# Attention and mixture-of-experts kernel: value products as two 64-key matmuls on two row tiles, value splitting over two groups, list tiles with a step of 2

## The chip, the cores and the metric

The kernel runs on one core of a Trainium2 chip, as one program. The metric is the device time of one execution in microseconds (us), lower is better. Besides the plain runs there is one execution taken with the hardware profiler; its rows are what the text argues from. The engines are called as the profile calls them: PE (matrix multiply), PEld (its weight loads), DVE (vector), ACT (scalar), POOL and SP (mostly issuing DMAs).

## What is computed

```python
# B, S, D = 8, 2496, 256; z is (B, S, 64); E = 8 experts, F = 1024
scores = z @ z.transpose(0, 2, 1) / S
out    = np.maximum(scores, 0.0) ** 2 @ v
x      = (u * out).reshape(B * S, D)
logits = x @ w_gate                       # (B*S, E)
# greedy: the (token, expert) pairs in falling order of logit; a token takes the first expert
# that has room left (capacity B*S/E = 2496 rows each)
y[rows of e] = np.maximum(x[rows of e] @ w1[e], 0.0) @ w2[e]
```

All products are made with float32 values split into a high and a low part of type fp32r (a reduced float32 that PE takes in one pass), three matmuls for each: high by high, high by low, low by high.

## The kernel before

**Attention, the first part.** A batch has 2496 queries and as many keys. Queries go in 5 groups of 512 (the last of 448), keys in 20 tiles of 128 (the last of 64). One pass of one group over one key tile is a *step* here; a group has 20 steps, the stage 8 x 5 x 20 = 800. The steps are numbered through, n, and one loop (lines 967 to 986) writes the program: at step n it writes the scores of step n+4, the square of n+2, and so on, and work that is due now and then is held in a table, `todo`, under the number of the step (lines 913 to 952). For a step:

- `scores` (L782), every fourth step for four key tiles at once: z has 64 columns, so these matmuls contract over 64 rows, and two of them are written one after the other for the upper and the lower 64 rows of the PE array, into two PSUM banks. Three such pairs make the scores of two key tiles; a visit of `scores` is 6 pairs, 12 matmuls.
- `rectify` and `square` on ACT (tiles r, a), `split_hi` (tile hi; for three steps of five on ACT, for two on DVE, L803) and `split_lo` (tile lo, DVE, L812).
- `av` (L825, L827, L828): for each half d of v's 256 columns three matmuls over all 128 keys, vh by hi, vh by lo, vl by hi, into the bank `acc{d}`. There are two banks of each d, so that a group writes one while the other is read. The last step of a group has 64 keys and needs no lo of its own; it has two matmuls for each d.

At a group's end `take_acc` copies the two banks to SBUF (`at0` on ACT, `at1` on DVE, L836 and L834); two steps on, `turn_back` (L848) turns them on PE with 8 transposes over all 128 rows; `post_mul` (L859, tile xs) multiplies by u; and `post_logits` (L876, tile lt) makes the gate's logits on DVE, 32 instructions for each group. For the next batch z is turned (`z_turn`, two transposes each, 5 times in a batch's third group) and v is split into vh (ACT) and vl (DVE) by `split_v` (L763, L764), one key tile in each step of the batch's last group. [...] After the eighth batch comes the second part.

**Routing and experts, the second part.** Expert by expert, a threshold search (`hist`) finds the rows of the expert, the list of these rows is built, rows are gathered, and the two layers run on PE. The list of an expert is a product of one-hot tiles (`oa`, `hl`, `ob` in `route`): for each of 156 columns one matmul (L431) whose stationary operand is `obs[c][:, n, :, r]` and whose moving operand is `hl[:, n, :, :, r]`. The tiles have the columns in runs of QW = 4 innermost, so that DVE can work on runs; PE thus reads every fourth element of a bfloat16 tile. The routing of expert k+1 is written between the matmuls of expert k.

**What sets the order.** The engines each take their own instructions in program order. That order is not the order in which the Python loop calls: the tile framework sorts instructions when it builds the program, within what data and buffers allow. So the place of an instruction on its engine is read from the built program.

Of the kernel before, what the change touches and what calls it, by code (L numbers as in the profile page):

```python
# [8 lines left out]
F32 = mybir.dt.float32  # L9
# [4 lines left out]
AF = mybir.ActivationFunctionType  # L14
# [81 lines left out]
def moe(tc, xd, first, jp, identf, w1, w2, out, B, S, cp):  # L96
    nc = tc.nc
# [22 lines left out]
    with ExitStack() as ctx:  # L120
# [77 lines left out]
        nc.vector.tensor_copy(idl, idh_i)  # L198

        CB = JP // 4  # L200
        QW = 4
        QN = CB // QW
        slot = rp.tile([128, 128, QW], BF, name="slot")
        nc.gpsimd.iota(slot, pattern=[[1, 128], [0, QW]], base=0, channel_multiplier=0,  # L204
# [444 lines left out]
def attention(tc, u, v, z, w_gate, xd, identf, made, first, scale):  # L649
# [15 lines left out]
    with ExitStack() as ctx:  # L665
# [8 lines left out]
        def load_gate():  # L674
            wgb = wk.tile([128, E, D], F32, name="wgb", bufs=1)
            for h in range(2):
                wg = wk.tile([128, DH, 128 * E // 2], F32, name="wg", tag="xs")
                wg = wg.rearrange("p a b -> p (a b)")
                nc.sync.dma_start(wg, bass.AP(tensor=w_gate.tensor, offset=w_gate.offset + h * 128 * E,
                                              ap=[[0, 128], [1, 128 * E]]))  # L680
                with in_turn(0):
                    nc.vector.tensor_copy(wgb[:, :, h * 128:(h + 1) * 128], wg.rearrange("p (d e) -> p e d", e=E))
            wgt = wk.tile([128, DH, E], F32, name="wgt", bufs=1)
            nc.sync.dma_start(wgt, w_gate.rearrange("(h p) e -> p h e", h=DH))
            WG.update(rows=wgb, cols=wgt)
# [83 lines left out]
        def width(g):  # L769
            return min(512, S - 512 * g)  # L770
# [43 lines left out]

        def av(n):
            b, g, kt = seq[n]
            if kt == 0:
                ACC[b, g] = [ps.tile([128, 512], F32, name=f"acc{d}") for d in range(2)]
            last = kt == NT
            h, l = HI.pop(n), LO.pop(n, None)  # L820
            for d in range(2):
                o = ACC[b, g][d][:, :width(g)]
                c = slice(d * 128, (d + 1) * 128)
                vh, vl = VH[b, kt][:, c], VL[b, kt][:, c]
                nc.tensor.matmul(o, vh, h, start=(kt == 0), stop=False)  # L825
                if not last:
                    nc.tensor.matmul(o, vh, l, start=False, stop=False)  # L827
                nc.tensor.matmul(o, vl, h, start=False, stop=last)  # L828

        def take_acc(b, g, d):  # L830
            t = wk.tile([128, 512], F32, name=f"at{d}", bufs=2)[:, :width(g)]
            o = ACC[b, g][d][:, :width(g)]
            if d:
                nc.vector.tensor_copy(t, o)  # L834
            else:
                nc.scalar.activation(t, o, AF.Copy)  # L836
            AT[b, g, d] = t

        def turn_back(b, g):
            for half in range(2):  # L840
                p = ps.tile([128, 512], F32, name="sc", bufs=SCB)
                for i in range(2 * half, 2 * half + 2):
                    c = slice(i * 128, (i + 1) * 128)
                    if 4 * g + i == NT:
                        c = slice(i * 128 + TL - 128 * (b % 2) - TL * (1 - b % 2), i * 128 + TL)
                    for d in range(2):
                        o = p[:c.stop - c.start, (i % 2) * D + d * 128:(i % 2) * D + (d + 1) * 128]
                        nc.tensor.transpose(o, AT[b, g, d][:, c], identf)  # L848
                ACC[b, g][half] = p

        def post_mul(b, g, half):
            if half == 0:
                XS[b, g] = wk.tile([128, 4, D], F32, name="xs")
            acc = ACC[b, g][half].rearrange("p (i d) -> p i d", d=D)
            full = NT - 4 * g - 2 * half
            cuts = [(0, 2, 128)] if full >= 2 or b % 2 else [(0, full, 128), (full, 2, TL)]
            for i, j, n in cuts:
                c = slice(2 * half + i, 2 * half + j)
                nc.vector.tensor_mul(XS[b, g][:n, c], acc[:n, i:j], UR[b, g][:n, c])  # L859
            if half == 1:  # L860
                xs = XS[b, g]
                n = min(4, NT - 4 * g)
                nc.sync.dma_start(xd[b * S:b * S + NT * 128].rearrange("(p i) d -> p i d", i=NT)[:, 4 * g:4 * g + n],
                                  xs[:, :n])
                if n < 4:
                    nc.sync.dma_start(xd[b * S + NT * 128:(b + 1) * S], xs[TL * (b % 2):TL * (b % 2) + TL, n])
# [38 lines left out]
            best_expert(nc, wk, first, slice(lo, hi), eq[:, :hi - lo])  # L905
            order_keys(nc, first, slice(lo, hi))

        todo = {}

        def at(n, f, *a):  # L910
            todo.setdefault(n, []).append((f, a))
# [4 lines left out]
        for b in range(B):  # L916
            for g in range(NQ):
                n0 = (b * NQ + g) * KT
                m0 = n0 + KT
                t = m0 + (0 if m0 == B * NQ * KT else 2)  # L920
                for d in range(2):
                    at(m0, take_acc, b, g, d)
                at(t, turn_back, b, g)
                for d in range(2):
                    at(t + 1, post_mul, b, g, d)
                for e in range(4 * E if m0 < B * NQ * KT else 0):
                    at(t + 2 + e * (KT - 7) // (4 * E), post_logits, b, g, e // E, e % E)
                if b or g:
                    at(n0 - 3, load_u, b, g)
            n0 = b * NQ * KT  # L930
            if b == B - 1:
                at(B * NQ * KT + 2, last_logits, b, NQ - 1)
                at(B * NQ * KT + 3, settle, b * NT + 4 * (NQ - 1), (b + 1) * NT)
                at(B * NQ * KT + 3, settle, B * NT, J)
            if b:
                for g in range(NQ):
                    m = n0 - 3 * KT + 4 * g
                    at(m - 4, load_z, b, g)
                    at(m, z_turn, b, g)
                    at(n0 - KT + 4 * g - 8, load_v, b, g)  # L940
                at(n0 - 3 * KT + 4 * NQ + 2, swap_z, b, slice(0, KT * 128))
                for kt in range(KT):
                    at(n0 - KT + kt, split_v, b, kt)
            else:
                for kt in range(KT):
                    at(kt - 4, split_v, 0, kt)
                for g in range(1, NQ):
                    at(4 * g - LA - 1, z_turn, 0, g)
                    at(4 * g - LA, swap_z, 0, slice(512 * g, 512 * g + 512))
                    if g >= 3:  # L950
                        at(4 * g - 13, load_z, 0, g)
                        at(4 * g - 11, load_v, 0, g)
# [14 lines left out]
        for n in range(-LA, N + 4 * E):  # L967
            if n == 2:
                early.close()
            if n % 4 == 0 and 0 <= n + LA < N:  # L970
                scores(n + LA)
            if 0 <= n + LA < N:
# [2 lines left out]
                square(n + 2)  # L975
            if 0 <= n + 1 < N:
                split_lo(n + 1)
            if 0 <= n + 2 < N:
                split_hi(n + 2)
            for k in sorted(k for k in todo if k < n):  # L980
# [31 lines left out]
```

## Time and profile before

| | us |
|---|---|
| runs shown | 2620.06 (median of 3, 2619.9 to 2625.03) |
| profiled execution, its own time | 2624.11 |
| its span (first to last instruction) | 2622.1 |
| attention, last product of the last group issued | 1479 |
| attention, PE clock granted | full |

The span and what lies around it (2.0 us) make the profiled execution's time, 4 us over the median of the runs shown. The prediction quotes the rows. In a timeline a row is: start in us, duration in us, engine, line, operation, out<-in, tile of the PE array (rows*columns), shape, count. The durations of PE's rows overlap, since matmuls are pipelined: what one costs is read from the starts of two that follow each other. The same holds for DVE and ACT, where a start can lie some 0.08 us ahead of the end of the instruction in front of it.

### The profile page before, as it was taken

The numbers are of one execution on the slowest core, as the hardware profiler recorded it, in microseconds if no ns is written. First come the engines' busy times: TensorE is split into PE (matmuls) and PEld (weight loads), VectorE is DVE, ScalarE is ACT, GpSimd is POOL, SyncE is SP. The second block draws the span as 40 slices with busy tenths as digits, with TensorE's granted clock in tenths as the row PEclk, the third lists the DMA queues.
The fourth block names the chain that finished last, engine by engine and source line by source line (L and its number), as shares of the span: only waits on it lengthen the run. The fifth ranks groups of instructions, "written<-read, shape, count | busy, mean of one in ns | idle before, by whom it ended". The sixth has DMA issues, their size and how long they took to land.

```text
span 2622.1 us, 44527 instructions
## 1 busy us (share of the span) xinstructions
PE 2540.4 (97%) x16035; PEld 2091.9 (80%) x16035; DVE 1992.1 (76%) x6127; ACT 1523.7 (58%) x2941; POOL 361.0 (14%) x506
## 2 busy tenths in 40 slices
PE   8999999999999999999999749999999999999998
PEld 6777777777777777777777638888989898999997
DVE  6888788887898888887888768958595969696322
ACT  7788787787787887878877412323233333233332
POOL 2000000000000000000000003233333333333331
PEclk9999999999999999999999859999999999999999
DMA  4121220220121211212100011212121212121110
GB/s 139 41 79 48 57 62 32 63 72 31 49 72 39 66 58 37 72 48 57 39 25 25 16 41 49 69 41 67 41 71 39 74 39 73 39 90 55 45 43 24
DMA packets 71645, 139.60 MB, mean 53 GB/s; under 512 B 12160, under 2 KB 39680, under 8 KB 71424
## 3 DMA queue, kind: packets, MB, share of 16 engines
q1 hardware_dynamic: 56320, 95.84, 12.2%
q0 software_dynamic: 15104, 40.91, 5.0%
q8 instruction: 126, 2.06, 0.3%
q14 instruction: 95, 0.78, 0.1%
HBM read 85.60 MB, written 40.89 MB: 48 GB/s over the span
## 4 chain that ended last, share of the span: by engine, by line
PE 82%; DVE 12%; ACT 3%; issue 2%; DMA 1%; POOL 0%; POOLq 0%; ACTq 0%; SPq 0%; DVEq 0%
PE acc L825 13%; PE acc L828 11%; PE acc L827 11%; PE sc L782 11%; PE hp L514 5%; PE y L545 5%; PE y L547 5%; PE y L546 5%; PE hp L515 5%; PE hp L516 5%; DVE lt L876 3%; DVE lo L812 2%; PE srch L431 2%; PE srch L230 2%; PE xp L499 1%
## 5 line engine op out<-in xcount | busy, mean ns | idle before, releaser
L812 DVE TENSOR_TENSOR lo<-a,hi 128x512 fp32r<-128x512 f32 (+1 forms) x760 | 508.4, 673 | 191.9 <-ACT hi L801 186.5
L825 PE MATMUL acc<-hi,vh 128*128 128x512 f32 (+1 forms) x1600 | 645.9, 404 | 1.8 <-ACT hi L801 1.8
L828 PE MATMUL acc<-hi,vl 128*128 128x512 f32 (+1 forms) x1600 | 617.9, 386 | 0.0
L827 PE MATMUL acc<-lo,vh 128*128 128x512 f32 (+1 forms) x1520 | 589.2, 388 | 0.5 <-DVE lo L812 0.2
L795 ACT ACTIVATE a<-r 128x512 f32<-128x512 f32 (+1 forms) x800 | 492.0, 631 | 145.4 <-DVE lo L812 145.4
L533 ACT ACTIVATE hh<-hp 128x512 fp32r<-128x512 f32 (+1 forms) x320 | 188.0, 588 | 562.2 <-PE hp L516 478.3
L876 DVE SCALAR_TENSOR_TENSOR lt<-xs,wgb 128x256 bf16<-128x256 f32 x1248 | 464.0, 415 | 0.5
L790 ACT ACTIVATE r<-sc 128x512 f32<-128x512 f32 (+1 forms) x800 | 426.9, 589 | 62.9 <-PE sc L782 60.5
L825 PEld LDWEIGHTS acc<-hi,vh 128*128 128x128 f32 x1600 | 300.7, 188 | 121.5 <-issue 39.5
L545 PE MATMUL y<-w2h,hh 128*128 128x256 f32 (+1 forms) x1280 | 365.1, 285 | 0.0
L546 PE MATMUL y<-w2l,hh 128*128 128x256 f32 (+1 forms) x1280 | 361.6, 283 | 0.0
L828 PEld LDWEIGHTS acc<-hi,vl 128*128 128x128 f32 x1600 | 300.9, 188 | 57.3 <-issue 0.9
L827 PEld LDWEIGHTS acc<-lo,vh 128*128 128x128 f32 x1520 | 286.3, 188 | 51.0 <-DVE lo L812 5.0
L801 ACT ACTIVATE hi<-a 128x512 fp32r<-128x512 f32 (+1 forms) x480 | 292.7, 622 | 57.8 <-PE acc L828 55.8
L514 PE MATMUL hp<-xh,w1h 128*128 128x512 f32 (+2 forms) x646 | 262.0, 406 | 0.3 <-ACT xh L507 0.3
L515 PE MATMUL hp<-xl,w1h 128*128 128x512 f32 (+2 forms) x646 | 250.4, 388 | 0.0
L516 PE MATMUL hp<-xh,w1l 128*128 128x512 f32 (+2 forms) x646 | 249.2, 386 | 0.0
L545 PEld LDWEIGHTS y<-w2h,hh 128*128 128x128 f32 (+1 forms) x1280 | 240.0, 188 | 10.3
L546 PEld LDWEIGHTS y<-w2l,hh 128*128 128x128 f32 (+1 forms) x1280 | 240.0, 187 | 9.1
L578 POOL DMA_INDIRECT out_dram<-y,idx x160 | 181.5, 1134 | 389.0 <-ACT y L572 341.5
L446 POOL DMA_INDIRECT xg<-xd,idx x160 | 160.9, 1006 | 397.9 <-PE xp L499 140.6
L204 POOL IOTA slot<- 128x512 bf16 x1 | 1.2, 1211 | 1455.1 <-DVE nrem L278 1455.1
(1144 smaller groups left out, 3793.1 us busy)
## 6 DMA issues: line engine op xcount, KB each, us to landing
vr<-in_v_dram SPq DMA_DIRECT2D x32, 512.0 KB, 3.7
ur<-in_u_dram SPq DMA_DIRECT2D x32, 512.0 KB, 4.4
xd<-xs SPq DMA_DIRECT2D x32, 512.0 KB, 2.9
wr<-in_moe_w_dram SPq DMA_DIRECT2D x32, 512.0 KB, 5.2
zh<-zh SPq DMA_DIRECT2D x14, 320.0 KB, 4.0
zl<-zl SPq DMA_DIRECT2D x14, 320.0 KB, 6.1
zin<-in_z_dram SPq DMA_DIRECT2D x31, 128.0 KB, 2.0
vr<-in_v_dram SPq DMA_DIRECT2D x8, 384.0 KB, 3.3
```

What stands on the lines that cost most here:

```text
L514: nc.tensor.matmul(p[:, c], wh, xh, start=(d == 0), stop=False)
L515: nc.tensor.matmul(p[:, c], wh, xl, start=False, stop=False)
L516: nc.tensor.matmul(p[:, c], wl, xh, start=False, stop=(d == DH - 1))
L545: nc.tensor.matmul(o, h[:, c], wh, start=first, stop=False, skip_group_check=True)
L546: nc.tensor.matmul(o, h[:, c], wl, start=False, stop=False, skip_group_check=True)
L790: recent["r"] = nc.scalar.activation(r, p, AF.Relu, scale=scale)
L795: nc.scalar.activation(a, R.pop(n), AF.Square)
L812: recent["l"] = nc.vector.tensor_sub(l, a, h.bitcast(F32))
L825: nc.tensor.matmul(o, vh, h, start=(kt == 0), stop=False)
L827: nc.tensor.matmul(o, vh, l, start=False, stop=False)
L828: nc.tensor.matmul(o, vl, h, start=False, stop=last)
L876: nc.vector.scalar_tensor_tensor(t[r], XS[b, g][r, i], 1.0, WG["rows"][r, e], op0=OP.mult, op1=OP.mult, accum_out=lg[r, j, e:e + 1])
```

## The change

`av` now makes each product over 128 keys as two matmuls over 64 keys, one for the upper 64 rows of the array and one for the lower, written one after the other into two banks of their own: four banks, `acc{d}{s}`, one buffer of each. At a group's end `take_even` copies the banks of s = 0 to SBUF (both on ACT) and `add_odd` adds the banks of s = 1 to them (both on DVE). The calls of `split_v` are spread over 34 steps in place of 20, and the loads of v are written earlier; `at` and `xs` have one buffer less. In the second part QW is 2.

```diff
-        QW = 4
+        QW = 2
...
         def av(n):
             b, g, kt = seq[n]
+            w = width(g)
             if kt == 0:
-                ACC[b, g] = [ps.tile([128, 512], F32, name=f"acc{d}") for d in range(2)]
+                ACC[b, g] = [[ps.tile([128, 512], F32, name=f"acc{d}{s}", bufs=1) for s in range(2)] for d in range(2)]
...
             for d in range(2):
-                o = ACC[b, g][d][:, :width(g)]
                 c = slice(d * 128, (d + 1) * 128)
-                vh, vl = VH[b, kt][:, c], VL[b, kt][:, c]
-                nc.tensor.matmul(o, vh, h, start=(kt == 0), stop=False)
-                if not last:
-                    nc.tensor.matmul(o, vh, l, start=False, stop=False)
-                nc.tensor.matmul(o, vl, h, start=False, stop=last)
-
-        def take_acc(b, g, d):
-            t = wk.tile([128, 512], F32, name=f"at{d}", bufs=2)[:, :width(g)]
...
+                for v, x in ((VH, h), (VH, l), (VL, h)):
+                    for s in range(2) if x is not None else ():
+                        r = slice(64 * s, 64 * s + 64)
+                        nc.tensor.matmul(ACC[b, g][d][s][:, :w], v[b, kt][r, c], x[r], start=(kt == 0 and v is VH and x is h),
+                                         stop=(last and v is VL))
+
+        def take_even(b, g):
+            for d in range(2):
+                t = wk.tile([128, 512], F32, name=f"at{d}", bufs=1)[:, :width(g)]
+                nc.scalar.activation(t, ACC[b, g][d][0][:, :width(g)], AF.Copy)
+                AT[b, g, d] = t
+
+        def add_odd(b, g):
+            for d in range(2):
+                t = AT[b, g, d]
+                nc.vector.tensor_add(t, t, ACC[b, g][d][1][:, :width(g)])
...
-                    at(n0 - KT + 4 * g - 8, load_v, b, g)
+                    at(n0 - KT - 6 + 7 * g, load_v, b, g)
...
-                    at(n0 - KT + kt, split_v, b, kt)
+                    at(n0 - KT + 2 + 17 * kt // 10, split_v, b, kt)
...
         for n in range(-LA, N + 4 * E):
+            if n in ends:
+                take_even(*ends[n])
             if n % 4 == 0 and 0 <= n + LA < N:
                 scores(n + LA)
...
                 split_lo(n + 1)
+            if n in ends:
+                add_odd(*ends[n])
```

**Where a group begins, on PE.** First before: the last pair of a visit of `scores`, then the first step's products, three for each d.

```order
L782 MATMUL sc_1612<-zh_120,zl_121 128x512
L782 MATMUL sc_1613<-zh_120,zl_121 128x512
L825 MATMUL acc0_1628<-hi_1584,vh_147 128x512 [waits Activation_49]
L827 MATMUL acc0_1628<-lo_1596,vh_147 128x512
L828 MATMUL acc0_1628<-hi_1584,vl_148 128x512
L825 MATMUL acc1_1629<-hi_1584,vh_147 128x512
L827 MATMUL acc1_1629<-lo_1596,vh_147 128x512
L828 MATMUL acc1_1629<-hi_1584,vl_148 128x512
```

And the same place in the changed kernel.

```order
L782 MATMUL sc_1368<-zh_120,zl_121 128x512
L782 MATMUL sc_1369<-zh_120,zl_121 128x512
L827 MATMUL acc00_1386<-hi_1326,vh_147 128x512 [waits Activation_49]
L827 MATMUL acc01_1387<-hi_1326,vh_147 128x512 [waits DVE_49]
L827 MATMUL acc00_1386<-lo_1344,vh_147 128x512
L827 MATMUL acc01_1387<-lo_1344,vh_147 128x512
L827 MATMUL acc00_1386<-hi_1326,vl_148 128x512
L827 MATMUL acc01_1387<-hi_1326,vl_148 128x512
L827 MATMUL acc10_1388<-hi_1326,vh_147 128x512 [waits Activation_49]
L827 MATMUL acc11_1389<-hi_1326,vh_147 128x512 [waits DVE_49]
```

Each product is now two, and the first into each of the four banks waits for the engine that empties that bank of the group before.

**The same place on DVE, in the changed kernel.** Here the two additions (L839) stand, and before there was one copy (L834) in place of the first of them and nothing in place of the second.

```order
L812 TENSOR_TENSOR lo<-a,hi 128x512 x3
L839 TENSOR_TENSOR at_789<-at_789,acc_213 128x512
L803 CAST hi<-a 128x512
L839 TENSOR_TENSOR at_791<-at_791,acc_215 128x512
L812 TENSOR_TENSOR lo<-a,hi 128x512
```

A split of another step (L803) came to stand between the two additions.

**Steps 6 to 10 of a group, on DVE.** Before: xs of the group before is made when its transposes are done, and the 32 lt of that group follow, between the lo of steps 6, 7, 8 and 9 (the four rows of L812, in that order).

```order
L859 TENSOR_TENSOR xs<-sc,ur 128x512 x2
L876 SCALAR_TENSOR_TENSOR lt,lg<-xs,wgb 128x256 x3
L812 TENSOR_TENSOR lo<-a,hi 128x512
L876 SCALAR_TENSOR_TENSOR lt,lg<-xs,wgb 128x256 x2
L812 TENSOR_TENSOR lo<-a,hi 128x512
L876 SCALAR_TENSOR_TENSOR lt,lg<-xs,wgb 128x256 x6
L803 CAST hi<-a 128x512
L876 SCALAR_TENSOR_TENSOR lt,lg<-xs,wgb 128x256
L812 TENSOR_TENSOR lo<-a,hi 128x512
L803 CAST hi<-a 128x512
L876 SCALAR_TENSOR_TENSOR lt,lg<-xs,wgb 128x256
L812 TENSOR_TENSOR lo<-a,hi 128x512
```

In the changed kernel, from the same xs on; behind the last row come the lo of step 9, 6 more lt and the lo of step 10.

```order
L863 TENSOR_TENSOR xs<-sc,ur 128x512 x2
L880 SCALAR_TENSOR_TENSOR lt,lg<-xs,wgb 128x256 x3
L812 TENSOR_TENSOR lo<-a,hi 128x512
L880 SCALAR_TENSOR_TENSOR lt,lg<-xs,wgb 128x256 x3
L812 TENSOR_TENSOR lo<-a,hi 128x512
L880 SCALAR_TENSOR_TENSOR lt,lg<-xs,wgb 128x256 x13
L803 CAST hi<-a 128x512
L880 SCALAR_TENSOR_TENSOR lt,lg<-xs,wgb 128x256
L812 TENSOR_TENSOR lo<-a,hi 128x512
L880 SCALAR_TENSOR_TENSOR lt,lg<-xs,wgb 128x256 x5
L803 CAST hi<-a 128x512
L880 SCALAR_TENSOR_TENSOR lt,lg<-xs,wgb 128x256
```

The 32 lt of a group moved forward: all stand before the lo of step 10 now, where 15 of them did, and the other 17 stood between the lo of steps 10 and 15. In the other groups it is much the same (a batch's last group has splits of v between them, 4 of which stand before the lo of step 11). Of the 20 splits of v, 16 stand on DVE among the lo of a batch's last group and 4 among those of the next, as before. In the second part the order on every engine is unchanged.

More of the change, by code (lines that the diff above doesn't have):

```diff
@@ L676, in load_gate @@
             for h in range(2):
-                wg = wk.tile([128, DH, 128 * E // 2], F32, name="wg", tag="xs")
+                wg = wk.tile([128, DH, 128 * E // 2], F32, name="wg", tag="xs", bufs=2)
                 wg = wg.rearrange("p a b -> p (a b)")
@@ L821, in av @@
             for d in range(2):
-                o = ACC[b, g][d][:, :width(g)]
                 c = slice(d * 128, (d + 1) * 128)
-                vh, vl = VH[b, kt][:, c], VL[b, kt][:, c]
-                nc.tensor.matmul(o, vh, h, start=(kt == 0), stop=False)
-                if not last:
-                    nc.tensor.matmul(o, vh, l, start=False, stop=False)
-                nc.tensor.matmul(o, vl, h, start=False, stop=last)
-        def take_acc(b, g, d):
-            t = wk.tile([128, 512], F32, name=f"at{d}", bufs=2)[:, :width(g)]
[L832 to L837, printed above, removed]
+                for v, x in ((VH, h), (VH, l), (VL, h)):
[12 more added lines that the diff above has]
+                nc.vector.tensor_add(t, t, ACC[b, g][d][1][:, :width(g)])
         def turn_back(b, g):
+            banks = []
             for half in range(2):
@@ L848, in turn_back @@
                         nc.tensor.transpose(o, AT[b, g, d][:, c], identf)
-                ACC[b, g][half] = p
+                banks.append(p)
+            ACC[b, g] = banks
         def post_mul(b, g, half):
             if half == 0:
-                XS[b, g] = wk.tile([128, 4, D], F32, name="xs")
+                XS[b, g] = wk.tile([128, 4, D], F32, name="xs", bufs=2)
             acc = ACC[b, g][half].rearrange("p (i d) -> p i d", d=D)
@@ L906, in settle @@
             order_keys(nc, first, slice(lo, hi))
-        todo = {}
+        todo, ends = {}, {}
         def at(n, f, *a):
@@ L920, in attention @@
                 t = m0 + (0 if m0 == B * NQ * KT else 2)
-                for d in range(2):
-                    at(m0, take_acc, b, g, d)
+                ends[m0] = (b, g)
                 at(t, turn_back, b, g)
```

## The prediction

> **What bounds the kernel now.** I read the page first, then the windows of one whole batch, then the timelines of PE and DVE where the change acts.
>
> ```profile
> span 2622.1 us, 44527 instructions
> PE 2540.4 (97%) x16035; PEld 2091.9 (80%) x16035; DVE 1992.1 (76%) x6127; ACT 1523.7 (58%) x2941; POOL 361.0 (14%) x506
> ```
>
> Then the windows; after the stretch and its length stand the busy times of PE, PEld, DVE and ACT.
>
> ```profile
> 571.41:608.60 37.19, 37.19 (x188) 27.97 (x186) 31.42 (x112) 29.74 (x60) 0.00 (x0) 1.00 0.13 40
> 608.60:645.35 36.75, 36.75 (x189) 27.85 (x187) 28.56 (x97) 28.41 (x55) 0.00 (x0) 1.00 0.09 29
> 645.35:684.00 38.65, 38.52 (x199) 28.84 (x197) 32.56 (x106) 31.63 (x65) 0.00 (x0) 1.00 0.21 58
> 684.00:720.41 36.41, 36.41 (x188) 27.85 (x186) 29.16 (x98) 27.84 (x55) 0.00 (x0) 1.00 0.21 52
> 720.41:754.16 33.75, 33.73 (x188) 27.66 (x187) 31.98 (x111) 29.80 (x71) 0.00 (x0) 1.00 0.33 97
> ```
>
> These are the five groups of the fourth batch. PE is busy throughout at clock 1.00, so attention is paced by PE. But DVE is busy 28.6 to 32.6 us of each group too: it has 2 to 8 us to spare, and its place in the order matters. The batch takes 182.75 us.
>
> **Part 1: what PE gains.** Around one visit of the scores:
>
> ```profile
> 643.21 0.39 PE L825 MATMUL acc<-hi,vh 128*128 128x512 f32 x1
> 643.44 0.39 PE L828 MATMUL acc<-hi,vl 128*128 128x512 f32 x1
> 643.76 0.50 PE L782 MATMUL sc<-zh 64*128 64x512 f32 x2
> 644.09 0.40 PE L782 MATMUL sc<-zl,zh 64*128 64x512 f32 x2
> ...
> 645.02 0.39 PE L782 MATMUL sc<-zh,zl 64*128 64x512 f32 x2
> 645.35 0.50 PE L825 MATMUL acc<-hi,vh 128*128 128x512 f32 x1
> 645.68 0.40 PE L827 MATMUL acc<-lo,vh 128*128 128x512 f32 x1
> ```
>
> Two 128-row products start 0.23 apart (0.227 on average). The scores are already pairs of two 64-row matmuls, the form that the change gives to the products: from 644.09 to 645.02 are four pairs, 0.2325 each. A product in the new form thus costs 0.232, some 5 ns more than now; 4720 of them, +24 us. Against this, the step into the visit takes 0.32, the next 0.33, the step out 0.33, the next 0.33, each about 0.1 more than its like: 0.39 a visit, 78 us over 200 visits. With both sides in 64-row form that goes.
>
> It comes back in part at the transposes, which use all 128 rows and now stand between 64-row products:
>
> ```profile
> 612.59 0.39 PE L828 MATMUL acc<-hi,vl 128*128 128x512 f32 x1
> 612.82 1.03 PE L848 MATMUL sc<-identf,at 128*128 128x128 f32 x8
> 613.61 0.48 PE L825 MATMUL acc<-hi,vh 128*128 128x512 f32 x1
> 613.93 0.40 PE L827 MATMUL acc<-lo,vh 128*128 128x512 f32 x1
> ...
> 646.61 0.40 PE L828 MATMUL acc<-hi,vl 128*128 128x512 f32 x1
> 646.84 0.38 PE L743 MATMUL sc<-identf,zin 128*128 128x128 f32 x2
> 646.98 0.48 PE L825 MATMUL acc<-hi,vh 128*128 128x512 f32 x1
> 647.30 0.40 PE L827 MATMUL acc<-lo,vh 128*128 128x512 f32 x1
> ```
>
> From the last product before to the second behind it is 1.34 with 8 transposes and 0.69 with 2: less two products, 0.89 and 0.24. Entering is free now (0.23), and the second product behind already waits 0.32. So of the 0.39 a visit can add between nothing and all; I take 0.26, the parts that aren't there yet (0.1 each at entry, at the second transpose, and nearly so at exit): 1.15 and 0.50 a visit. There are some 78 such visits, +20 us (0 to 30).
>
> [...]
>
> PE alone would then need, for a 512-wide group, 148 pairs (118 products, 30 of scores) x 0.232 + 1.15 = 35.5 us, and 38.0 for the third group with its five z visits. With 448 queries a pair is 64 columns of 0.44 ns shorter, 0.204: 31.3.
>
> **Part 2: a new wait where a group begins.** The four banks have one buffer each, so the first product of a group waits until the last group's are emptied.
>
> ```profile
> 643.52 1.30 DVE L812 TENSOR_TENSOR lo<-a,hi 128x512 fp32r<-128x512 f32 x2 [1.22 <-ACT hi L801]
> ...
> 643.91 0.58 ACT L836 ACTIVATE at<-acc 128x512 f32<-128x512 f32 x1
> ...
> 644.73 0.68 DVE L834 COPY at<-acc 128x512 f32<-128x512 f32 x1
> ...
> 645.33 0.42 DVE L803 CAST hi<-a 128x512 fp32r<-128x512 f32 x1
> ```
>
> Count from the start T of the group's last product (643.44). ACT copies at T+0.5 and T+1.0. The two lo keep DVE until T+1.29, where at1 is copied now and the first addition will stand (0.68 with its tail): done T+1.97. PE, with six pairs of scores in between, wants that bank at T+1.62: 0.4 late. Then the cast (0.33) and the second addition, done T+2.9; PE wants it three pairs after the first, at T+2.7: 0.2 more. Behind the waiting matmul stand all products of the group. I take 0.6 a group, bounded by 0 (both lo done sooner) and 1.2 (twice that). Groups of PE alone: 36.1, 38.6, 31.9. That would still be a gain: 179 a batch.
>
> **Part 3: what DVE's new order costs.** Its own row times in the group from 608.60:
>
> ```profile
> 613.45 1.29 DVE L859 TENSOR_TENSOR xs<-sc,ur 128x512 f32<-128x512 f32 x2
> 614.66 0.41 DVE L876 SCALAR_TENSOR_TENSOR lt<-xs,wgb 128x256 bf16<-128x256 f32 x1
> 615.00 0.08 DVE L876 DVE_READ_ACCUMULATOR lt<-xs,wgb 128x1 f32 x1
> ...
> 615.69 0.68 DVE L812 TENSOR_TENSOR lo<-a,hi 128x512 fp32r<-128x512 f32 x1
> 616.30 0.41 DVE L876 SCALAR_TENSOR_TENSOR lt<-xs,wgb 128x256 bf16<-128x256 f32 x1
> ...
> 619.67 0.42 DVE L803 CAST hi<-a 128x512 fp32r<-128x512 f32 x1
> 620.00 0.42 DVE L876 SCALAR_TENSOR_TENSOR lt<-xs,wgb 128x256 bf16<-128x256 f32 x1
> 620.35 0.69 DVE L812 TENSOR_TENSOR lo<-a,hi 128x512 fp32r<-128x512 f32 x1
> ...
> 624.05 0.50 PE L825 MATMUL acc<-hi,vh 128*128 128x512 f32 x1
> ```
>
> Start to start: the two xs 1.21, an lt 0.345 (three from 614.66 to 615.69), a lo 0.61, a cast 0.33. Adding up the old order from 613.45 (2 xs, 12 lt, a cast, two lo) gives 620.35 for the start of step 8's lo, and the row says the same: in this stretch DVE waits for nothing. PE began step 8 at 624.05, 3 us after that lo was done. That lead was the cover.
>
> In the new order 20 lt, not 12, stand before the lo of step 8 and 32, not 15, before that of step 10. From the start of xs:
>
> - lo of step 8 done: 1.21 + 20 x 0.345 + 0.33 + 3 x 0.61 = 10.3
> - lo of step 9: + 6 x 0.345 + 0.33 + 0.61 = 13.3
> - lo of step 10: + 6 x 0.345 + 0.61 = 16.0
>
> PE runs meanwhile. xs can start about 0.35 before PE's step 3, since it needs the first four transposes (now 0.16 before, and one more change of form comes in between). From there PE reaches the product with lo of step 8 after 30 pairs of steps 3 to 7, 12 of scores and one more: 0.35 + 43 x 0.232 = 10.3, just in time. It wants step 9's six pairs later, at 11.7, and waits 1.6; from 13.3 it wants step 10's at 14.7 and waits 1.3. Step 11's lo follows 0.6 later and the lead grows again, with no lt left. So 2.9 us a group are lost. Nothing later gives them back, as PE has no slack.
>
> The other groups by the same sum: the third has z visits that slow PE by 1.0 in the stretch, so 1.9. The first also has the small routing instructions of the last batch before step 11's lo, some 1.5 us (DVE is busy 2.9 longer in its window than in the next, 1.4 of it four splits of v at 0.34, like an lt, which is as wide); less the 0.8 that PE's step leaves over DVE's lo, 3.7. The last (448 wide, DVE's lo scaled to 0.53) has 30 lt and 4 splits of v before step 11's lo, 16.7 us against 12.8 of PE: 3.9. The splits of v stay where they were, 16 and 4; spreading the calls changes nothing that I can price.
>
> Groups: 36.1 + 3.7 = 39.8, 36.1 + 2.9 = 39.0, 38.6 + 1.9 = 40.5, 39.0, 31.9 + 3.9 = 35.8: a batch 194.1, +11.4. Over 39 groups (not the very first, which starts on loads) that is 7.8 batches: +89 us.
>
> **Part 4: the lists.**
>
> ```profile
> 1612.57 0.42 PE L230 MATMUL srch<-mask,oh 128*128 128x48 bf16 x10
> 1612.83 0.48 PE L516 MATMUL hp<-xh,w1l 128*128 128x512 f32 x1
> ...
> 1668.75 1.81 PE L431 MATMUL srch<-hl,ob 128*128 128x40 bf16 x40
> 1670.40 0.36 PE L545 MATMUL y<-w2h,hh 128*128 128x256 f32 x1
> ```
>
> Forty list matmuls take 1.65 us, 41 ns each, with a step of 4; the search's ten, on dense operands and wider, take 26 ns each. A step of 2 lies between, 0 to 15 ns a matmul. It makes each read element 4 bytes apart, as the float32 operands above are, which stream 512 columns in 227 ns without loss: I take 14. PE is full there (97% over the span) in the 7 routings that run beside the experts: 7 x 156 x 14 ns = -15 us. The first routing waits for DVE, not PE: 0.
>
> [...]
>
> Sum: 2624.1 + 89 - 15 = 2698 beside the profiled execution; the median shown lies 4 lower, so **2694**.
>
> **Rivals.** (a) *The lt run stays covered*: xs starts early enough for DVE to hold its 3 us lead. Then PE alone counts: 179 a batch, -3.9, times 7.8 is -31, and -15: 2578, 2574 by the median. It decides at step 8's lo: 3 us more lead there and the waits go. Against it: xs waits for transposes that PE issues behind step 2, as before. (b) *The step of 4 costs nothing*: 2709. (c) *The pairs do not stay side by side* in runs of 30 and more, which this trace doesn't show beyond six: at 0.25 a pair DVE's chain hides a part, but some +55 us come on top, 2750; one after the other, which is the change not doing what it says, 4720 x 0.22 gives over 3600. The x2 in rows of 0.40 us speaks against that. (d) *Half of the waits vanish* because the boundary and the transposes cost nothing and xs comes sooner: 2640 and, at the edge, no change.
>
> **Chances.** Forecast 0.68, (b) 0.12, (c) 0.06, (a) 0.08, (d) 0.06. Unknowns: pair time 0.227 to 0.236, -20 to +18; transposes -13 to +10; boundary -23 to +23; lists 0 to +15. Not all at once: 2640 to 2745, which holds the forecast, (b), and most of (d). A measurement here tells 0.2% (5 us) from no change: faster 0.09, same 0.04, slower 0.87.
>
> **What would show it.** Right: PE waits for lo (L812) at steps 9 and 10 of nearly every group, groups of 39 to 40 us; PE waits for at (L839) where a group begins; pairs 0.23 apart; no 0.3 steps around the scores, but some around the transposes; list matmuls at 26 to 30 ns. Wrong: groups near 36 us with no wait for lo, or pairs 0.25 or more apart.

## The result, and the profile after

| | before | changed |
|---|---|---|
| median of the runs (range) | 2620.5 us (2619.9 to 2625.0) | 2818.4 us (2812.8 to 2821.8) |
| ratio to before, 95% interval | | 1.0752 (1.0734 to 1.0770) |
| last product of attention starts | 1479.0 us | 1691.6 us |
| from there to the end | 1143.1 us | 1128.3 us |
| mean batch, second to seventh | 182.7 us | 211.1 us |

The changed kernel is slower by 198 us, where 74 were forecast and at most 125 allowed for. The second part gained the 15 us forecast. The whole miss lies in attention: it lost 213 us, not 89.

First the page of the changed kernel: the header, the busy times, the granted clock by fortieths of the span, the shares of the chain that ended last, and three groups of instructions.

```profile
span 2819.9 us, 53926 instructions
PE 2587.9 (92%) x20755; PEld 2136.7 (76%) x20755; DVE 2027.0 (72%) x6167; ACT 1548.2 (55%) x2981; POOL 362.9 (13%) x506
PEclk9999998999998999999999995899999999999999
PE 51%; DVE 32%; ACT 13%; issue 3%; DMA 1%; POOL 0%; POOLq 0%; ACTq 0%; DVEq 0%; SPq 0%
L827 PE MATMUL acc<-hi,vh 64*128 64x512 f32 (+1 forms) x3200 | 751.2, 404 | 66.2 <-ACT at L833 28.0
L827 PE MATMUL acc<-lo,vh 64*128 64x512 f32 (+1 forms) x3040 | 704.5, 405 | 66.7 <-DVE lo L812 65.3
L795 ACT ACTIVATE a<-r 128x512 f32<-128x512 f32 (+1 forms) x800 | 483.1, 630 | 299.1 <-DVE lo L812 298.3
```

PE fell from 97 to 92% of the span. It waits ahead of two kinds of products: those with hi (mostly for the banks' copies, at L833 and L839, and for casts of hi) and those with lo (for DVE, L812). A third of the chain is DVE now; before it was an eighth:

```profile
PE 82%; DVE 12%; ACT 3%; issue 2%; DMA 1%; POOL 0%; POOLq 0%; ACTq 0%; SPq 0%; DVEq 0%
```

And the clock row has eights inside attention, where before had none.

The windows of the fourth batch's five groups show where it went. After the stretch and its length stand the busy times of PE, PEld, DVE, ACT and POOL, then the granted clock, the DMA share and GB/s.

```profile
648.42:693.65 45.23, 41.36 (x304) 31.62 (x305) 31.57 (x111) 29.00 (x57) 0.00 (x0) 0.90 0.10 33
693.65:734.88 41.23, 38.58 (x304) 29.57 (x304) 29.36 (x97) 28.83 (x55) 0.00 (x0) 0.96 0.08 27
734.88:778.32 43.44, 40.15 (x314) 30.40 (x314) 33.80 (x107) 32.70 (x65) 0.00 (x0) 1.00 0.18 49
778.32:817.43 39.11, 36.57 (x305) 28.58 (x305) 29.39 (x98) 28.33 (x55) 0.00 (x0) 1.00 0.21 53
817.43:859.78 42.35, 35.47 (x306) 28.59 (x304) 34.25 (x116) 31.74 (x74) 0.00 (x0) 0.99 0.26 77
```

Forecast were 39.8, 39.0, 40.5, 39.0 and 35.8. The fourth group hits its forecast to 0.1. The first is 5.4 too long, the last 6.5, the third 2.9, and the second 2.2. The granted clock is 0.90 in the first group and 0.96 in the second.

What the fourth group loses is near what was forecast. This is the timeline of DVE and PE around its steps 9 and 10 (start, duration, engine, line; in brackets the wait ahead and who ended it):

```profile
797.14 0.69 DVE L812 TENSOR_TENSOR lo<-a,hi 128x512 fp32r<-128x512 f32 x1
797.75 0.42 DVE L880 SCALAR_TENSOR_TENSOR lt<-xs,wgb 128x256 bf16<-128x256 f32 x1
797.89 0.50 PE L827 MATMUL acc<-lo,vh 64*128 64x512 f32 x2 [0.45 <-DVE lo L812]
...
799.82 1.29 DVE L812 TENSOR_TENSOR lo<-a,hi 128x512 fp32r<-128x512 f32 x2
800.57 0.50 PE L827 MATMUL acc<-lo,vh 64*128 64x512 f32 x2 [1.02 <-DVE lo L812]
```

Between the lo of step 9 and that of step 10 DVE makes six lt, and PE stands still. Counted by the starts of PE's products, step 9 loses 1.6 us here (half of it for hi, whose cast stands behind lt too) and step 10 1.3, as forecast; step 8 loses 0.3. In the third group it is another tile: there PE waits less for lo (0.7 us a group) than for zl (2.4), the low part of the turned z, which DVE also makes behind the lt. From 400 to 1400 us:

```profile
PE sc L782 <- DVE zl L750: 10.5, 10, 1.2
```

The forecast had only lo there. The rows of PE's form changes also came out as forecast:

```profile
783.24 0.61 PE L827 MATMUL acc<-hi,vl 64*128 64x512 f32 x2
783.78 1.09 PE L851 MATMUL sc<-identf,at 128*128 128x128 f32 x8
784.80 0.50 PE L827 MATMUL acc<-hi,vh 64*128 64x512 f32 x2
785.14 0.39 PE L827 MATMUL acc<-lo,vh 64*128 64x512 f32 x2
...
786.07 0.40 PE L827 MATMUL acc<-hi,vl 64*128 64x512 f32 x2
786.30 0.39 PE L782 MATMUL sc<-zh 64*128 64x512 f32 x2
786.53 0.39 PE L782 MATMUL sc<-zl,zh 64*128 64x512 f32 x2
```

From products into scores (786.07 to 786.30 to 786.53) no step of 0.3 is left: 0.23 each, nearer to 0.227 than to the 0.232 forecast. Around the transposes there are more of them: from the last product ahead (783.47, the second of the two in the row at 783.24) to the second behind (785.14) it is 1.67, less two products 1.22 (forecast 1.15, before 0.89).

### The profile page after: what moved, and what is told of

Read it like the earlier page. It is cut to its first block, busy times and chain, and to the rows that moved or that the text cites. A ratio compares the mean times of both kernels' runs of the same rounds, so it can differ in the third digit from the quotient of the medians.

```text
span 2819.9 us, 53926 instructions
## 1 busy us (share of the span) xinstructions
PE 2587.9 (92%) x20755; PEld 2136.7 (76%) x20755; DVE 2027.0 (72%) x6167; ACT 1548.2 (55%) x2981; POOL 362.9 (13%) x506
## 4 chain that ended last, share of the span: by engine, by line
PE 51%; DVE 32%; ACT 13%; issue 3%; DMA 1%; POOL 0%; POOLq 0%; ACTq 0%; DVEq 0%; SPq 0%
PE acc L827 15%; DVE lt L880 14%; DVE lo L812 7%; PE y L545 5%; PE hp L514 5%; PE y L547 5%; PE y L546 5%; ACT a L795 5%; PE hp L515 5%; PE hp L516 5%; ACT r L790 4%; ACT hi L801 3%; PE sc L782 3%; DVE xs L863 2%; PE srch L230 2%
## 5 line engine op out<-in xcount | busy, mean ns | idle before, releaser
L827 PE MATMUL acc<-hi,vh 64*128 64x512 f32 (+1 forms) x3200 | 751.2, 404 | 66.2 <-ACT at L833 28.0
L827 PE MATMUL acc<-lo,vh 64*128 64x512 f32 (+1 forms) x3040 | 704.5, 405 | 66.7 <-DVE lo L812 65.3
L812 DVE TENSOR_TENSOR lo<-a,hi 128x512 fp32r<-128x512 f32 (+1 forms) x760 | 507.4, 677 | 302.0 <-ACT hi L801 294.5
L827 PE MATMUL acc<-hi,vl 64*128 64x512 f32 (+1 forms) x3200 | 716.5, 392 | 0.0
L795 ACT ACTIVATE a<-r 128x512 f32<-128x512 f32 (+1 forms) x800 | 483.1, 630 | 299.1 <-DVE lo L812 298.3
L827 PEld LDWEIGHTS acc<-hi,vh 64*128 64x128 f32 x3200 | 379.3, 190 | 189.3 <-ACT at L833 42.0
L827 PEld LDWEIGHTS acc<-lo,vh 64*128 64x128 f32 x3040 | 355.7, 190 | 161.5 <-DVE lo L812 117.4
L880 DVE SCALAR_TENSOR_TENSOR lt<-xs,wgb 128x256 bf16<-128x256 f32 x1248 | 455.0, 423 | 0.5
L790 ACT ACTIVATE r<-sc 128x512 f32<-128x512 f32 (+1 forms) x800 | 425.0, 587 | 19.5 <-PE sc L782 18.9
L827 PEld LDWEIGHTS acc<-hi,vl 64*128 64x128 f32 x3200 | 379.5, 190 | 51.3
```

What stands on the lines that cost most here:

```text
L790: recent["r"] = nc.scalar.activation(r, p, AF.Relu, scale=scale)
L795: nc.scalar.activation(a, R.pop(n), AF.Square)
L812: recent["l"] = nc.vector.tensor_sub(l, a, h.bitcast(F32))
L827: nc.tensor.matmul(ACC[b, g][d][s][:, :w], v[b, kt][r, c], x[r], start=(kt == 0 and v is VH and x is h), stop=(last and v is VL))
L880: nc.vector.scalar_tensor_tensor(t[r], XS[b, g][r, i], 1.0, WG["rows"][r, e], op0=OP.mult, op1=OP.mult, accum_out=lg[r, j, e:e + 1])
```

## What the runs were to settle

Theory A: DVE's new order (32 lt ahead of the lo of step 10) is the loss, and the waits also pull PE's clock down. Theory B: the single banks, emptied where a group begins, are the loss. Theory C: the splits of v hold ACT and DVE up in a batch's last group. The last group of the changed kernel speaks for C (who waited for whom; sum, times and longest, in us):

```profile
ACT a L795 <- DVE lo L812: 10.4, 8, 4.4
DVE vl L764 <- ACT vh L763: 7.2, 7, 1.5
```

DVE waits for vh, which ACT makes; ACT waits in front of its a for a buffer, which DVE's lo would free; and that lo stands behind the vl that waits. Two engines that each work in order take turns at standing still. That the splits bring this about is so far an argument from the rows; a run below moves them.

The first four runs and the last two were on chips where before took 2621.0 and 2623.5 us. The six between were on two others, where before took 2662.7 and 2665.0. As far as the traces show, the difference lies behind attention (1167 to 1177 us there in place of 1127, while the fourth group of the fourth batch takes 36.24 us both in lt_v_pinned on the first chip and in settle_moved on another). So I compare ratios and groups; a time "on the first chip" is an estimate, the ratio times 2621. Groups are means over the second to seventh batch unless a row is shown.

## First runs: one part undone at a time

**lt_pinned.** Each lt is held behind the lo ahead of it.

```diff
-            nc.vector.scalar_tensor_tensor(t[r], ...)
+            with tc.issue_after(recent["l"].ins):
+                nc.vector.scalar_tensor_tensor(t[r], ...)
```

> The changed kernel, with each lt held behind the lo that is written last ahead of it, so that DVE makes 2 or 3 lt a step from step 4 to step 18, as they are written. Theory A (DVE's run of lt makes lo late, and the waits pull PE's clock down): no PE wait for lo at steps 8 to 10, no stretch at clock 0.5 after the first batch, groups of 36 to 37 us, a batch of 178 to 184: 2560 to 2620 us. Theory B (the single banks and their copies at a group's end cost the time): the waits for at (L833, L839) stay, groups of 39 to 45 us, 2750 to 2820. Theory C (the splits of v lock ACT and DVE together in a batch's last group): g1 and g3 at 36 to 37, but g4 stays near 42 and g0 near 45: 2660 to 2720.

2694.4 us, ratio 1.0277 (1.0260 to 1.0294). The fourth batch:

```profile
605.37:647.25 41.88, 38.66 (x305) 29.58 (x305) 31.70 (x111) 29.27 (x57) 0.00 (x0) 0.96 0.11 35
647.25:683.86 36.61, 35.85 (x304) 28.56 (x304) 29.53 (x97) 29.08 (x55) 0.00 (x0) 1.00 0.09 30
683.86:723.93 40.07, 39.31 (x314) 29.71 (x314) 34.07 (x107) 32.73 (x65) 0.00 (x0) 1.00 0.19 53
723.93:760.18 36.25, 35.57 (x305) 28.55 (x305) 29.37 (x97) 28.53 (x55) 0.00 (x0) 1.00 0.23 57
760.18:799.63 39.45, 35.27 (x304) 28.64 (x305) 34.41 (x116) 32.19 (x74) 0.00 (x0) 1.00 0.27 82
```

124 us come back, 16.2 a batch, and the two plain groups stand at 36.2 to 36.8. So undoing A alone gives more than any other single run, and B in its strong form falls. But the first group (42.3 in the mean) and the last (39.4) stay long. At 2694 us it lies outside A's forecast and inside C's, though both groups are shorter than C had them (45 and 42). And of B something stays. What PE waits for most, from 400 to 1400 us, is now the banks:

```profile
PE acc L827 <- ACT at L833: 27.3, 26, 2.6
PE acc L827 <- DVE at L839: 10.8, 26, 0.4
PE acc L827 <- DVE lo L812: 8.4, 29, 0.4
```

**lt_v_pinned.** The splits of v are held back as well, so that they really lie in two groups; in the changed kernel the scheduler had put most of them back into one.

```diff
-            with in_turn(b):
+            with in_turn(0):
                 nc.scalar.activation(h, src, AF.Copy)
                 nc.vector.tensor_sub(l, src, h.bitcast(F32))
```

> As lt_pinned, and each split of v is held behind the last r on ACT and the last lo on DVE too, so that the 20 splits really lie in two groups: 11 among the lo of the last group and 9 among those of the next. Theory A: as lt_pinned to within 10 us, since DVE has room for the splits in either place. Theory C: g4 and g0 fall by 3 to 8 us each against lt_pinned, 40 to 90 us in all. Theory B: 2750 to 2820.

2670.0 us, ratio 1.0181 (1.0164 to 1.0198): 24 less, more than A's 10 and less than C's 40. The last group falls from 39.4 to 35.0, as C said, but the first stays at 42.6 and the second rises from 36.8 to 37.6. So C is right for one of its two groups.

**old_form_lt_early.** The old form of the products, with the calls of post_logits written so early that lt stands as in the changed kernel.

```diff
-                    at(t + 2 + e * (KT - 7) // (4 * E), post_logits, ...)
+                    at(t + 2 + (e > 2) + (e > 5) + (e > 18) + (e > 24), post_logits, ...)
```

> The kernel before, 128-row products and double banks, with the calls of post_logits written at steps 4 to 8 of a group, so that all 32 lt stand before the lo of step 10 as in the changed kernel. Theory A: the order alone costs most of the loss: PE waits for lo at steps 8 to 10, groups of 39 to 43 us, stretches at clock 0.5, 2700 to 2800 us. Theory B: the order is covered by slack, 2610 to 2640.

2726.6 us, ratio 1.0398 (1.0381 to 1.0415). The order alone costs the old form 106 us. Its second and fourth group, 36.75 and 36.41 in the prediction's windows, take

```profile
649.45:688.52 39.07, 37.34 (x188) 27.69 (x187) 28.62 (x97) 28.70 (x55) 0.00 (x0) 1.00 0.08 27
...
730.02:768.76 38.74, 37.01 (x188) 27.69 (x186) 29.25 (x98) 28.12 (x55) 0.00 (x0) 1.00 0.20 49
```

2.3 us more each. From 24 us on the clock stays at 1.00 through the whole of attention, against the expectation; the last section has a reason that fits.

**old_lists_step2.** The kernel before with QW = 2 alone.

> The kernel before with QW = 2 alone. If the step of 4 costs the list matmuls 14 ns each: 2603 to 2608 us, list matmuls of 26 to 30 ns, all of the gain behind the attention. If the step costs nothing: 2618 to 2623.

2606.7 us, ratio 0.9951 (0.9934 to 0.9968). Forty list matmuls now:

```profile
1664.84 1.18 PE L431 MATMUL srch<-hl,ob 128*128 128x40 bf16 x40
1665.86 0.36 PE L545 MATMUL y<-w2h,hh 128*128 128x256 f32 x1
```

1.02 us from start to start, 26 ns each where they were 41. Attention is unchanged (182.75 a batch).

## Second runs: what is left beside the order

**settle_moved.** In lt_v_pinned the first group is the odd one; DVE has the routing block of the batch before (settle) at step 15 there, where lo is ready 0.7 to 1.4 us ahead of PE in the two steps before, and PE waits for it from there on. It is moved to step 3 of the second group, where lo is at least 4 us ahead.

```diff
-            at(((b + 1) * NQ + 2) * KT, settle, b * NT, (b + 1) * NT)
+            at(((b + 1) * NQ + 1) * KT + 3, settle, b * NT, (b + 1) * NT)
...
+            with tc.issue_after(recent["l"].ins):
                 best_expert(...)
                 order_keys(...)
```

> As lt_v_pinned, and settle (the small routing instructions of the batch before, on DVE at step 15 of the first group there) is written at step 3 of the second group and held behind the lo ahead of it, where lo has a lead of 4 us. Theory D (the first group is long because that block uses up DVE's lead of 1.5 to 2 us at step 15): the first group falls from 41.9 to 37 to 38 us, the second stays below 38: 2635 to 2650 us. Rival (the first group is long because of the splits of v and of the clock at its start): the first group stays above 40: 2662 to 2675.

Ratio 1.0094 (1.0065 to 1.0122), which is 2645 on the first chip: as expected. The first group falls from 42.6 to 38.9, 0.9 less than expected, and the second, which has the block now, from 37.6 to 36.9. The windows of the first group in the fourth batch, of lt_v_pinned and of this run:

```profile
592.90:634.54 41.64, 38.05 (x305) 28.56 (x305) 34.35 (x119) 31.50 (x65) 0.00 (x0) 1.00 0.20 63
```

```profile
580.52:619.59 39.07, 37.39 (x304) 29.76 (x304) 32.44 (x107) 31.66 (x64) 0.00 (x0) 0.96 0.21 67
```

DVE has 12 instructions and 1.9 us less there (x119 to x107), and the group 2.6 less. The block cost more than its own time.

**rings_deeper.** As settle_moved, with hi in 6 buffers for 4, lo in 5 for 4, a in 4 for 3.

> As settle_moved, with more buffers: hi 6 for 4, lo 5 for 4, a 4 for 3, so that ACT and DVE may run further ahead of PE. Theory D (what PE still waits for in the groups is a short lead): the last group falls from 34.9 to 32 to 34 and the first to 37, 2600 to 2630. Rival (what is left is the boundary and the transposes, which more lead doesn't touch): within 6 us of settle_moved.

Ratio 0.9968 (0.9954 to 0.9982), 2612 on the first chip: as expected. The last group goes from 34.9 to 33.2, the first from 38.9 to 37.9, a plain one from 36.25 to 35.9. PE's waits for ACT's copies (L833), 21.2 us from 400 to 1400 us in settle_moved, are down to 0.8; those for DVE's additions rise from 10.7 to 18.9.

**rings_only.** The changed kernel with the deeper rings and nothing else.

> The changed kernel as it is (lt early, splits of v and settle where the scheduler puts them), with the deeper rings alone: hi 6, lo 5, a 4. Theory A (32 lt in a row are 11 us of DVE and outrun any lead of 3 to 5 us): the waits for lo shrink by some 1.4 us a group but stay, 2720 to 2790 us. Rival (lead is all that lacks): below 2680.

Ratio 1.0332 (1.0313 to 1.0351), 2708 on the first chip: between both. The plain groups fall to 36.6 and 36.8: there the rings leave one wait of 0.6 to 0.9 us at step 11 of the 2.9 us, where I had allowed for half. The first group still takes 42.7 and the third 43.9, 3.2 of it for zl. That is some 110 us less than the changed kernel, nearly as much as lt_pinned gave. More lead and a better order are two cures for one illness: DVE's bursts against the distance that the buffers let it run ahead.

**banks_in_turn.** As rings_deeper, with the last two and first two steps of a group made for d = 0 first.

```diff
+            if kt in (0, NT - 1):
+                return
+            steps = [n - 1, n] if kt in (1, NT) else [n]
             for d in range(2):
+                for m in steps:
...
```

> As rings_deeper, and PE makes the products of a group's last two steps and of its first two steps for d = 0 first and then for d = 1, so that the banks of d = 0 are done 5 pairs (1.1 us) earlier and those of d = 1 wanted 3 pairs later. If the wait where a group begins (1.06 us) is the time that ACT and DVE need to empty the banks after PE's last product: it falls by 0.7 to 1.0 a group, 25 to 40 us below rings_deeper. If ACT and DVE come late for other reasons (their own queues): less than 12 us below.

Ratio 0.9911 (0.9892 to 0.9931), some 15 us below rings_deeper: between the two cases. The timeline says why little came of it: at the end of the second group (last product at 638.06) both additions stand behind a cast and a lo on DVE.

```profile
638.72 0.42 DVE L803 CAST hi<-a 128x512 fp32r<-128x512 f32 x1
...
639.17 0.69 DVE L812 TENSOR_TENSOR lo<-a,hi 128x512 fp32r<-128x512 f32 x1
...
639.78 1.28 DVE L845 TENSOR_TENSOR at<-at,acc 128x512 f32<-128x512 f32 x2
```

**adds_first.** So lo and casts written after the additions are held behind them.

```diff
-                nc.vector.tensor_add(t, t, ACC[b, g][d][1][:, :width(g)])
+                recent["s"] = nc.vector.tensor_add(t, t, ACC[b, g][d][1][:, :width(g)])
...
+            with tc.issue_after(recent["s"].ins) if "s" in recent else nullcontext():
                 recent["l"] = nc.vector.tensor_sub(l, a, h.bitcast(F32))
...
```

> As banks_in_turn, and DVE's lo and casts written after the two additions are held behind them, so that at a group's end the additions come two lo and a cast (1.6 us of DVE) sooner in its order. If what is left of the wait where a group begins is DVE's own queue (the additions stand behind a cast and a lo there): the waits for at fall below 0.3 a group and the groups by 0.5 to 0.8 each, 15 to 30 us below banks_in_turn. Rival (DVE then idles for the banks and lacks the time later, lo comes late): as banks_in_turn or up to 20 us more.

Ratio **0.9847 (0.9831 to 0.9864)**, some 17 us below banks_in_turn, as expected: faster than before, and than the old form with the new lists. PE's waits for the banks are 0.8 us in all from 400 to 1400 us. Its fourth batch:

```profile
562.81:598.91 36.10, 35.72 (x304) 30.36 (x305) 32.53 (x108) 31.20 (x65) 0.00 (x0) 1.00 0.24 72
598.91:635.39 36.48, 36.37 (x309) 31.11 (x305) 31.87 (x111) 28.93 (x58) 0.00 (x0) 1.00 0.09 31
635.39:674.40 39.01, 38.74 (x313) 30.13 (x313) 32.84 (x105) 30.51 (x64) 0.00 (x0) 1.00 0.17 48
674.40:709.32 34.92, 34.92 (x307) 31.39 (x305) 29.86 (x98) 27.77 (x55) 0.00 (x0) 1.00 0.28 66
709.32:741.82 32.50, 32.29 (x307) 29.19 (x304) 30.17 (x107) 28.29 (x65) 0.00 (x0) 1.00 0.21 66
```

The fourth group is all PE now, 34.92 of 34.92, at clock 1.00; in before it was 36.41 of 36.41. That is what the new form is worth in this group: 1.5 us. The second group, which has the routing block now, gains 0.3.

**z_with_turn.** As adds_first, with each z visit next to a group's transposes.

```diff
-                    m = n0 - 3 * KT + 4 * g
+                    m = n0 - 5 * KT + KT * g + 2
...
-                at(n0 - 3 * KT + 4 * NQ + 2, swap_z, b, slice(0, KT * 128))
+                at(n0 - KT + 6, swap_z, b, slice(0, KT * 128))
```

> As adds_first, and each z visit stands next to the transposes of a group's end, one in each group, in place of five visits in the third group. If what a visit costs beyond its two transposes is the change between 64-row and 128-row form: a batch pays for 5 such changes in place of 10, the third group falls by 2.5 to 3.5 us, the others rise by 0.2 to 0.4 each, 8 to 20 us below adds_first. If the visits cost by their own transposes and waits: no change within 5 us.

Ratio 0.9905 (0.9888 to 0.9921), some 15 us above adds_first: a miss. The third group did fall by 2.7 (39.1 to 36.4), but each of the others rose by 1.2 to 1.7. Among the waits from 400 to 1400 us are new ones:

```profile
PE sc L782 <- DVE zl L750: 22.6, 24, 1.1
```

The scores that follow now wait for an sc bank that z's transposes hold until DVE has made zl; with 8 + 2 transposes and four scores near each other, the four banks that the kernel gives to sc (SCB) seem not to suffice. How much of the third group's 2.7 us was the change of form and how much the transposes' own time, no run separates.

## Last runs: the boundary alone, and a control

**banks_alone.** The changed kernel with the two boundary edits of banks_in_turn and adds_first, and all else as it is.

> The changed kernel with the wait at a group's start mended alone: the last two and first two steps of a group made for d = 0 first, and lo and casts written after the additions held behind them. lt, the splits of v and settle stay as in the changed kernel, and so do its buffers. Theory A (DVE's order is the main loss; a wait taken away at the start is met again where lo comes late): the waits for at fall, the waits for lo at steps 8 to 10 grow, 2760 to 2815 us against 2620 of before. Theory B (the boundary is the main loss): below 2700.

2790.0 us, ratio 1.0641 (1.0622 to 1.0660), 28 below the changed kernel, as A had it. From 400 to 1400 us the waits for the banks fall from 27.9 to 13.7 us, while those for lo rise from 39.9 to 43.3 and new ones appear. So mending the boundary alone gives little, since DVE's order takes back part of what is won. This doesn't make the boundary cheap: with lt in order the banks were the largest wait (lt_pinned).

**old_form_mended.** The old products and double banks, with everything else of adds_first.

> Control: 128-row products with double banks, as before, with everything of adds_first that isn't the new form: lists with a step of 2, lt, splits of v and settle in turn, deeper rings. If the new form itself gains once its waits are gone: only the lists gain here, as PE was 97% busy, ratio 0.992 to 0.997 to before (adds_first 0.985). If the gain of adds_first is that of the deeper rings and the order: ratio 0.983 to 0.988.

Ratio 0.9917 (0.9896 to 0.9938), 0.0034 below the lists alone: a little more than I had allowed for, since first and last group gain 0.4 each. A batch takes 181.9 us here and 179.0 in adds_first. Only those 3 us are the new form's own: 0.7, 0.4, 1.5 and 0.8 gained in the first, second, fourth and last group, and 0.5 lost in the third, where the z visits are.

## Why the prediction failed

*Part 1, PE's gain:* right. Pairs stand 0.227 apart (0.232 forecast), the steps around the scores are gone, and visits of transposes cost 1.22 (1.15 forecast) and, for z, 0.57 (0.50). In adds_first the fourth group takes 34.9; forecast for PE alone were 35.5. Steps of 0.3 us stand where the form changes: around the scores before (0.32 or 0.33, four a visit), around the transposes now (0.31 into them, 783.47 to 783.78, and 0.34 between the two products behind them, 784.80 to 785.14). What PE does in them the rows don't show.

*Part 2, the boundary:* right in kind, and less than half the size. In the fourth group's start of the changed kernel PE has these waits:

```profile
778.32 0.50 PE L827 MATMUL acc<-hi,vh 64*128 64x512 f32 x1 [0.20 <-ACT at L833]
778.49 0.69 DVE L839 TENSOR_TENSOR at<-at,acc 128x512 f32<-128x512 f32 x1
...
779.23 0.49 PE L827 MATMUL acc<-hi,vh 64*128 64x512 f32 x1 [0.41 <-DVE at L839]
```

While the odd bank is late, the even one's first product runs alone: its partner starts 0.91 behind it (778.32 and 779.23), where the two of a plain pair start 0.003 apart (783.013 and 783.016). The first step of that group takes 2.42 where a plain one takes 1.36 (six pairs): 1.06 more. Ahead of it PE waits for ACT's copy, which the sum had in time: the last pair of scores starts at 777.73, 0.59 before the first product in place of 0.23. That is 1.4 in all, where 0.6 was taken and 1.2 the bound, and this is one of the mildest boundaries: where a batch begins PE waits some 3 us for ACT's copy alone (2.82 ahead of 648.42, 2.83 ahead of 859.78).

*Part 3, the order of lt:* right in mechanism. Undoing it alone gives 2.9 in the fourth group (39.13 to 36.24; forecast 2.9) and 16.2 a batch (forecast 2.9 + 2.9 + 1.9 + 3.7 + 3.9 = 15.3). That the batch agrees so well is in part luck: the third group gives 3.3, mostly by the wait for zl that the sum didn't have, the last 2.9 where 3.9 were forecast, and by an estimate from the traces some 2.8 of the 16.2 are PE's clock (below).

*Part 4, the lists:* right, 41 to 26 ns, -15 us. So the step of 4 costs 15 ns on 26 here (forecast 14). The stationary and the moving operand change their step together, so which of them costs it is open.

*The rivals:* none came. DVE's lead did not cover the lt (a), the step of 4 did cost (b), pairs start 0.227 apart in long runs too (c), and the waits did not halve (d).

**The step that failed** is the floor on which part 3 was laid: "Groups of PE alone: 36.1, 38.6, 31.9. That would still be a gain: 179 a batch." With lt in order (lt_pinned) a batch takes 194.9, not 179: 42.3, 36.8, 40.1, 36.2 and 39.4. The plain groups are near it. The first and last are 6.2 and 7.5 above. 15.9 a batch over 7.8 batches is 124 us, the size of the miss (213 - 89).

Two steps of the prediction are in that figure. The first is its boundary term: 0.6 a group, 3.0 a batch, is 9.5 a batch in lt_pinned (what the steps between starts that ended a wait for the banks have beyond 0.227, or, at half clock, beyond twice that; measured there are 0.427 a pair, so this is an estimate), more than half of it at the two ends of a batch's first group, where ACT's copies come late. The second is that PE was taken for the pace of everything else once lt was out of the way: PE still waits 3.4 a batch for lo and hi, all of it in the first and last group, and half clock costs some 2.6. Together these are 12.5 of the 15.9 (6.5 above what was priced for the banks, 3.4 and 2.6); where the rest lies stays open.

Two pieces of work on DVE bring the long groups about. The splits of v: "the splits of v stay where they were; spreading the calls changes nothing that I can price" was wrong, since their places were the same but their neighbours were not. And the routing block: priced at 1.5 us in the first group, its move gave 3.8 there and 0.7 in the next (lt_v_pinned to settle_moved).

Undone one after the other, mean batch:

| | batch, us |
|---|---|
| changed kernel | 211.1 |
| lt in its steps | 194.9 |
| and splits of v in two groups | 191.6 |
| and settle where lo leads | 187.0 |
| and deeper rings | 183.2 |
| and d = 0 first at a group's ends | 181.4 |
| and additions ahead of lo | 179.0 |

The last row meets the forecast floor, 178.8, as a total; its groups lie between 1.2 below the forecast and 0.6 above it. Each step is worth its figure only after those above it, since the same lead is used up by all of them. Two things were missing from the sums. In the last group ACT and DVE wait for each other around the splits (ACT's and DVE's rows above), which a sum over DVE alone can't show. And the clock was taken as 1.00. The single buffers of at and xs stay in adds_first, so they cost little.

The clock: from 20 us on, 92 us of the changed kernel's attention run at 0.50. Pairs stand 0.427 apart there (650.39 to 652.52), nearly twice 0.227. Taking out what PE waited in them and halving the rest leaves some 42 us lost, a part of the figures above: about half of it where a batch begins, behind the long wait at the last group's end. lt_pinned has 41 us at 0.50 (some 20 lost), adds_first 6.8, all in its first batch, before none behind 24 us. These losses are estimates from the traces; no run changed the clock alone.

## What to carry to other kernels

When an engine off the critical path works in order, its sum of busy time says little: look at the longest run of its work that stands ahead of the one thing the pacing engine wants, and compare it with the lead that the buffers allow. A change that is worth some 1% in the end came out 7.5% slower here, more than half of it through an order that nobody meant to change and that cost the old form 106 us just as well; read the order that the scheduler made, hold it in place, and only then judge the new form. When double buffers go, add up the waits of every engine that empties them, at the worst place in the loop and not at a mild one. And don't lay a forecast on "engine X alone" for a stage where two other engines feed each other: walk through their queues together.

## What the hardware showed

In these traces PE's granted clock changes in slices of 3.41 us: from 24 us on, the changed kernel's attention has 19 stretches at 0.50, eleven of 3.41 us and eight of 6.83. It was halved after slices in which PE stood idle for about half the time or more (counted below), even where no single wait was long. The windows of the changed kernel, slice by slice, at a batch's end:

```profile
640.90:644.30 3.40, 3.40 (x34) 3.00 (x34) 2.16 (x6) 3.40 (x9) 0.00 (x0) 1.00 0.53 154
644.30:647.70 3.40, 1.30 (x11) 0.81 (x7) 2.09 (x4) 2.64 (x7) 0.00 (x0) 1.00 0.00 0
647.70:651.10 3.40, 2.52 (x9) 1.72 (x11) 3.40 (x8) 3.40 (x9) 0.00 (x0) 0.50 0.48 154
651.10:654.50 3.40, 3.40 (x18) 2.61 (x18) 1.14 (x3) 2.13 (x4) 0.00 (x0) 0.50 0.00 0
654.50:658.00 3.50, 3.50 (x29) 2.62 (x29) 1.95 (x4) 1.26 (x2) 0.00 (x0) 1.00 0.03 7
```

PE is busy 1.30 of 3.40 us in the second row; the next is at 0.50, with 9 matmul records where a full slice has 29 to 34. I divided the attention of all fourteen traces into such slices (from 40 us on, those at full clock) and took as idle what a step between matmul starts of over 0.34 us has beyond 0.227. Of 5796 slices with up to 1.4 us idle none was followed by a halved one, of 109 with 1.4 to 1.8 six, of 42 with 1.8 to 2.0 twenty-four, and of 53 with 2.0 or more all. In 38 of these 83 slices ahead of a halved one no single idle stretch was over 1.5 us. So about 2 us idle in one slice sufficed here, in one piece or in several. That fits old_form_lt_early, which kept its clock with at most 1.8 us idle in a slice.

In the profile of before a product of two fp32r operands is one record of PE: 1600 at L825, for 800 steps and two halves. The eight products of plain float32 operands at L893 leave 16.
